# Block-sparse attention and a GELU feed-forward on one Trainium2 core: a reordered first unit, and all keys of a query block side by side

## The chip, the cores and the metric

The kernel runs on one core of a Trainium2 chip. Its engines are TensorE (PE, matrix products; its weight loads are listed as PEld), VectorE (DVE), ScalarE (ACT), GpSimd (POOL) and SyncE (SP, which here only issues transfers). Each engine works through its own queue of instructions in order, and semaphores hold an instruction back until what it needs is there. The metric is the device time of one execution in microseconds (us), lower is better. The first such time is given as the median of three runs.

## What is computed

Attention over 4 batches, 8 heads, 768 positions and 64 values per head, in blocks of 32 positions (24 blocks). Query block *i* sees key block *j* if they are at most one apart, if either is the first or the last block, or if *j* is one of three blocks drawn for *i* (`sampled_blocks`). The result goes through a feed-forward pair of products with an exact GELU between them.

```python
scores = q @ k.T / sqrt(64)
mask = |bi - bj| <= 1  or  bi in {0, 23}  or  bj in {0, 23}  or  bj in sampled_blocks[bi]
attn = softmax(where(mask, scores, -1e9)) @ v            # (4, 8, 768, 64)
x    = attn.transpose(0, 2, 1, 3).reshape(3072, 512)
h    = x @ w_in                                          # (3072, 2048)
out  = (0.5 * h * (1 + erf(h / sqrt(2)))) @ w_out        # (3072, 512)
```

Inputs and output are float32; inside, the kernel works in bfloat16 with float32 sums.

## The kernel before

**Units.** The work is cut into eight units (b, hf): batch b and half hf of its 24 query blocks, so (0,0), (0,1), (1,0) up to (3,1). Line 594 loops over them. Each unit has three stages: attention for 384 positions, FFN1 (the product with w_in and the GELU) and FFN2 (the product with w_out). Attention of one unit is interleaved with FFN2 of the unit before it, whose products are cut into 24 pieces by a generator (`ffn2_pieces`, L437) and are called in between. FFN1 stands alone, in eight steps (`ffn1_step`, L429), and the loading and transposing of the next batch is hung on these steps. The order on each engine is the order in which the program text issues instructions; nothing reorders it later.

**Groups.** A unit's attention has eight groups (`unit_groups`, L303): its dense block (the first or last query block, which sees all 768 keys) as two groups of four heads each, and eleven sparse blocks in pairs, the last one alone. A group goes through scores (L312), exp (L343), transposes of the probabilities (L356), their eviction from PSUM by ACT (L369), the products with V (`stage_av`, L376) and the transposes of the result into xT (L411). The loop at L486 runs these in a pipeline: in step `it` it does the V products of group it - 1, the transposes of group it, the scores of group it + 2 and the exp of group it + 1, with pieces of FFN2 between. In the first unit, which has no FFN2 to mix in, V products lag by three.

**Keys.** kT holds all keys of a batch transposed; two buffers alternate. For a sparse query block the 256 keys are its window of three neighbouring blocks (96 columns, read straight from kT), the three sampled blocks and the first and last block (160 columns, copied side by side into `kg`). `k_globals` (L243) copies the first and last block for all eleven query blocks of a unit at once; `k_sampled` (L250) copies one sampled block with a block number held in a register, on DVE or on POOL. `block_numbers` loads such registers of an engine from a small list.

**Values.** V is written with a column of ones into a scratch tensor in device memory (`v_scratch`, L257), from which each query block fetches its 256 rows: a window of 96 rows (`v_window`, L282, four query blocks to one transfer in the first unit) and three sampled blocks of 32 rows (`v_sampled`, L264), issued on SP or on POOL by which of the two holds the register. Rows of the first and last block are copied in by `v_ends` (L270). In the first unit `first_rows` and `first_values` (L565, L568) make the scratch copy of V and issue all fetches of units (0,0) and (0,1), the rest of w_in, w_out and the keys of batch 1; the table `extra` (L591) says at which step of attention they run. Elsewhere the fetches of a unit are issued one unit ahead.

**PSUM.** Scores and FFN1 share two buffers of two banks (psA), transposes two (psT), FFN2 has one bank (psO), the V products one (psV). ACT and DVE take FFN2's three output tiles of a unit from psO (L447).

Of the kernel before, what the change touches and what calls it, by code (L numbers as in the profile page):

```python
# [11 lines left out]
BF16 = mybir.dt.bfloat16  # L12
# [8 lines left out]
def kernel(  # L21
# [68 lines left out]
    kTs = [const.tile([P, NPR, S], BF16, name=f"kT{i}") for i in range(2)]  # L90
    kg = const.tile([P, US, NPR, 160], BF16, name="kg")
    vg0s = [const.tile([P, US, VR], BF16, name=f"vg0{i}") for i in range(2)]
# [150 lines left out]
    def k_globals(b, p0=0, p1=NPR):  # L243
        for c0, blk in ((96, 0), (128, NB - 1)):
            nc.vector.tensor_copy(
                kg[:, :, p0:p1, c0:c0 + BL],
                kTs[b % 2][:, None, p0:p1, blk * BL:(blk + 1) * BL].to_broadcast(
                    [P, US, p1 - p0, BL]))

    def k_sampled(b, js, vals, copy):  # L250
        for j in js:
            for r in range(NR):
                if (j, r) in vals:
                    copy(kg[:, (j - 1) % US, :, BL * r:BL + BL * r],  # L254
                         kTs[b % 2][:, :, bass.ds(vals[j, r] * BL, BL)])
# [56 lines left out]
    def stage_scores(b, hf, grp):  # L312
        qT, kT = qTs[b % 2], kTs[b % 2]

        def product(out_, h, j, rhs):
            rows = slice(64 * (h % 2), 64 * (h % 2) + 64)
            nc.tensor.matmul(out_, lhsT=qT[rows, h // 2, j * BL:(j + 1) * BL], rhs=rhs[rows],  # L317
                             start=True, stop=True)
        A = psA.tile([P, 1024], F32, name="sc", tag="A")
        nm = small.tile([P, 4], F32, name="nm")  # L320
        if grp[0] == "sparse":
            js = grp[1:]
            A4 = A.rearrange("p (g j c) -> p j g c", j=2, g=2)
            for i, j in enumerate(js):
                for c0, c1 in ((0, 96), (96, 256)):
                    for hh in range(4):
                        rhs = (kT[:, hh, (j - 1) * BL:(j + 2) * BL] if c0 == 0
                               else kg[:, (j - 1) % US, hh, :])
                        for G in range(2):
                            product(A4[32 * hh:32 * hh + 32, i, G, c0:c1], 2 * hh + G, j, rhs)  # L330
            n = len(js)
            nc.vector.tensor_reduce(out=nm[:, 0:2 * n].rearrange("p (j g) -> p j g", g=2),  # L332
                                    in_=A4[:, 0:n], op=ALU.max, axis=AX.X, negate=True)
        else:
            _, j, G = grp
            for c0, c1 in ((0, 512), (512, 768)):
                for hh in range(4):
                    product(A[32 * hh:32 * hh + 32, c0:c1], 2 * hh + G, j, kT[:, hh, c0:c1])
            nc.vector.tensor_reduce(out=nm[:, 0:1], in_=A[:, 0:S], op=ALU.max, axis=AX.X,  # L339
                                    negate=True)  # L340
        st[grp] = (A, nm)
# [95 lines left out]
    def ffn2_pieces(b, hf):  # L437

        for t in range(UT // P):
# [6 lines left out]
            os = opool.tile([P, D_MODEL], F32, name="os")  # L446
            if t == 1:  # L447
                nc.vector.tensor_copy(os, op)
            else:
                nc.scalar.copy(os, op)  # L450
            row = b * S + hf * UT + t * P
# [24 lines left out]
    def attention(b, hf, filler, extra, steps=(), lag=1):  # L476
# [9 lines left out]
        for it in range(-1, n + lag + 1):  # L486
            if it == -1:
                pieces(2)
                stage_scores(b, hf, groups[1])
                stage_exp(groups[0])  # L490
                pieces(3)
            else:
# [23 lines left out]
        for f in steps:  # L516
# [8 lines left out]
    nc.vector.tensor_copy(rf, ids)  # L525
    k_list = numbers_list(ids, J0[5:], RS, POOL)
    k_pool = registers(k_list)
# [3 lines left out]
    lists = [numbers_list(vf, J0[:6], (0, 1), SP), numbers_list(vf, J0[6:], (0,), SP),  # L531
             numbers_list(vf, J1, (0, 1), SP)]
    v_pool = block_numbers(vf, J0[:6], (2,), POOL) | block_numbers(vf, J0[6:], (1, 2), POOL)
# [4 lines left out]
    def k_unit(hf, b, js):  # L538
        if hf:
            k_sampled(b, js, k_pool, nc.gpsimd.tensor_copy)  # L540
        k_sampled(b, js, k_dve, nc.vector.tensor_copy)
# [8 lines left out]
    banks = [(psA, "A"), (psA, "A"), (psO, "O"), (psA, "A")]  # L550
    for half in (0, 1):
        for pr in (2 * half, 2 * half + 1):
            prep_pair(0, "k", pr, pr != 2, bank=banks[pr])
            prep_pair(0, "q", pr, True, 0, 64)
        if half == 0:
            k_globals(0, 0, 2)
    k_globals(0, 2, 4)
    k_dve = block_numbers(ids, J0[:5], RS, DVE)
    stage_scores(0, 0, unit_groups(0)[0])
    k_sampled(0, J0[5:], k_pool, nc.gpsimd.tensor_copy)  # L560
    k_unit(0, 0, J0[:2])
    load_w_in(1)
    v_ends(0, 0, nc.gpsimd.tensor_copy)

# [3 lines left out]
    def first_values():  # L568
# [3 lines left out]
        for a in range(0, US, 4):  # L572
            v_window(0, 0, a, min(a + 4, US))
            for j in J0[a:a + 4]:
                for r in range(NR):
                    v_sampled(0, j, r)
            if a < 8:
                load_w_in(2 + a // 4)
        for hs in HALVES:
            load_q(0, hs, slice(64, P))  # L580
        for part in (0, 1):
            load_w_out(part)
        v_pool.update(block_numbers(vf, J1, (2,), POOL))
        for a in range(0, US, 4):
# [4 lines left out]
        for hs in HALVES:  # L589
            load_k(1, hs)  # L590
    extra = {-1: [first_rows], 0: [first_values, lambda: k_unit(0, 0, J0[2:4])],  # L591
             1: [lambda: k_unit(0, 0, J0[4:5])]}

    for u in range(-1, len(units)):
        nxt = units[u + 1] if u + 1 < len(units) else None
        filler = iter(())
        if u >= 0:
            b, hf = units[u]
            fresh = nxt is not None and nxt[1] == 0
            if u == 0:  # L600
                k_dve |= block_numbers(ids, J1, (2,), DVE)
                k_pool = block_numbers(ids, J1, (0, 1), POOL)
            if nxt and not fresh:
                k_unit(1, b, J1)
            if u == 1:
                v_rows(1, nc.vector.tensor_copy)
                v_scratch(1)
                v_ends(1, 0, nc.gpsimd.tensor_copy)
                for f in sum(v_fetch(1, 0), []):
                    f()  # L610
# [15 lines left out]
            else:  # L626
                steps, later = [], []
            steps = iter(steps)
            for s in range(KOUT // 2):
                if s == KOUT // 2 - 1 and nxt:  # L630
                    stage_scores(*nxt, unit_groups(nxt[1])[0])
                ffn1_step(2 * s)
                next(steps, lambda: None)()
                if u == 0 and 3 <= s < 7:
                    prep_pair(0, "q", s - 3, False, 64, P)
                if u == 0 and s == 6:
                    k_dve |= block_numbers(ids, J0[5:], RS, DVE)
                    for f in load_qk(1)[2:] + load_v(1):
# [3 lines left out]
                if fresh and s < 4:  # L642
                    for pr in (2 * (s % 2), 2 * (s % 2) + 1):
                        prep_pair(b + 1, "k" if s < 2 else "q", pr, s >= 2)
                    if s == 1:
                        k_globals(b + 1)
                        k_unit(0, b + 1, J0)
            for f in steps:
                f()
            if nxt:  # L650
                nc.scalar.activation(warm, identity[:, 0:1], AF.Exp)
            filler = ffn2_pieces(b, hf)
        if nxt is None:
# [35 lines left out]
```

## Time and profile before

| what | value |
|---|---|
| median of three runs | 353.23 us (348.99 to 356.44) |
| the profiled execution | 352.86 us, of which the span from the first to the last instruction is 351.2 us |
| mean granted PE clock | 0.917 of full speed |
| busy: PE | 294.2 us (84%), weight loads 176.4 us |
| busy: ACT | 212.2 us (60%) |
| busy: DVE | 188.1 us (54%) |
| busy: POOL | 131.3 us (37%) |
| chain that ended last | PE 67%, ACT 12%, DMA 7%, "issue" 7%, DVE 3% |
| score products (L317) | 704 of 96 columns, 704 of 160 columns, 128 dense |
| start of FFN1 in the first unit | 53.83 us |

A page of the profile covers one execution. An engine's busy share is the time in which it executes something; register loads, branches and the issuing of transfers do not count as busy. A low share does not mean slack where an engine waits for another that waits for it. The chain that ended last is followed back from the last instruction, at each step to what released it; it says which work set the end. "issue" in it is time in which an engine stood still although it waited for nothing that the profile shows. Groups of instructions carry the line of the kernel, the engine, the operation and the tiles (out<-in) with their shape.

### The profile page before, as it was taken

To read this page: it belongs to the slowest core of one execution; us is meant where nothing else is said; L and a number is where in the kernel's file an instruction comes from. 1 tells how busy PE (TensorE), PEld (TensorE's weight loads), DVE (VectorE), ACT (ScalarE), POOL (GpSimd) and SP (SyncE) were. 2 spreads that over 40 slices of the span, in tenths; PEclk is the share of its full clock that TensorE was granted. 3 is DMA by queue.
4 is the path that set the end of the run, shared out by engine and by line. 5 is a ranking of instruction groups with operands and counts; after the bars stand their busy time and mean duration, and the time that the engine had idled before them with its cause. 6 is when DMAs were issued, how large, how long until landed. Compare 5 with 4: busy or idle time off the path is not lost.

```text
span 351.2 us, 13168 instructions
## 1 busy us (share of the span) xinstructions
PE 294.2 (84%) x5228; PEld 176.4 (50%) x5284; DVE 188.1 (54%) x561; ACT 212.2 (60%) x452; POOL 131.3 (37%) x269
## 2 busy tenths in 40 slices
PE   5536649986999889987699999996999989988996
PEld 4324424544555454544455464554564555455575
DVE  7397332566475656347457586346574674277000
ACT  2357322486647856578537795586657894688440
POOL 8383751184517644196630240596400410000000
PEclk9656556999699989999899999999999999999999
DMA  7945999979448972679954021798270120000002
GB/s 111 196 66 169 203 235 223 171 103 182 71 165 189 194 174 79 215 132 219 161 140 104 2 72 57 223 170 174 74 192 20 38 69 33 0 34 34 30 20 73
DMA packets 43807, 42.27 MB, mean 120 GB/s; under 512 B 7969, under 2 KB 38690, under 8 KB 43746
## 3 DMA queue, kind: packets, MB, share of 16 engines
q0 software_dynamic: 22528, 17.55, 31.8%
q1 hardware_dynamic: 20786, 23.48, 23.7%
q8 instruction: 41, 0.67, 0.8%
q10 hardware_dynamic: 432, 0.39, 0.3%
q14 instruction: 20, 0.16, 0.2%
HBM read 45.63 MB, written 9.67 MB: 157 GB/s over the span
## 4 chain that ended last, share of the span: by engine, by line
PE 67%; ACT 12%; DMA 7%; issue 7%; DVE 3%; SPq 1%; POOL 1%; DVEq 1%; POOLq 0%
PE hp L433 25%; PE op L442 18%; PE tp L365 6%; ACT pp L350 5%; PE av L392 5%; PE sc L317 4%; PE pt L227 4%; DMA vg<-vscr 4%; PE op L466 3%; ACT ps L372 2%; ACT L510 2%; DMA qn<-in_q_dram 2%; PE tx L422 2%; ACT g L435 1%; DMA vscr<-vn 1%
## 5 line engine op out<-in xcount | busy, mean ns | idle before, releaser
L433 PE MATMUL hp<-xT,w_in_sb 128*128 128x384 bf16 x512 | 91.0, 333 | 3.1 <-ACT g L435 2.8
L442 PE MATMUL op<-w_out_sb,g 128*128 128x512 bf16 x280 | 83.5, 390 | 11.5 <-issue 7.2
L435 ACT ACTIVATE g<-hp 128x768 bf16<-128x768 f32 x64 | 51.9, 810 | 56.2 <-PE hp L433 56.2
L268 POOL DMA_DIRECT2D vg<-vscr x108 | 54.0, 503 | 78.4 <-issue 24.9
L332 DVE TENSOR_REDUCE nm<-sc 128x4 f32<-128x1024 f32 (+1 forms) x48 | 54.5, 1135 | 32.1 <-PE sc L317 20.6
L350 ACT ACTIVATE pp<-sc,nm 128x256 bf16<-128x256 f32 x176 | 70.3, 497 | 0.0
L433 PEld LDWEIGHTS <-w_in_sb 128*128 128x128 bf16 x512 | 49.6, 99 | 39.6 <-issue 9.4
L372 ACT COPY ps<-tp 128x256 int32<-128x256 int32 (+2 forms) x128 | 39.9, 352 | 38.6 <-PE tp L365 37.2
L365 PE MATMUL tp<-identity,pp 128*128 128x128 bf16 x448 | 43.8, 238 | 7.3 <-ACT pp L353 4.1
L365 PEld LDWEIGHTS <-pp 128*128 128x128 bf16 x448 | 33.5, 112 | 29.1 <-ACT pp L353 11.2
L254 POOL COPY kg<-kT 128x128 bf16 x106 | 26.1, 293 | 58.5 <-PE sc L317 51.8
L339 DVE TENSOR_REDUCE nm<-sc 128x1 f32<-128x768 f32 x16 | 15.3, 957 | 43.9 <-PE sc L317 40.2
L442 PEld LDWEIGHTS <-g 128*128 128x128 bf16 x336 | 24.7, 98 | 23.7 <-issue 7.2
L392 PEld LDWEIGHTS <-ps 128*32 128x32 bf16 x1792 | 20.2, 99 | 28.6 <-issue 14.7
L392 PE MATMUL av<-vg,ps 128*32 128x65 bf16 x1408 | 23.0, 202 | 13.7 <-DMA vg<-vscr 7.2
L317 PE MATMUL sc<-kT,qT 64*32 64x96 bf16 (+2 forms) x832 | 26.3, 237 | 0.9 <-DVE qT L241 0.3
L405 DVE TENSOR_TENSOR xh<-av,rec 128x256 bf16<-128x256 f32 (+1 forms) x64 | 22.9, 358 | 2.2
L425 DVE COPY xT<-tx 128x256 bf16<-128x256 bf16 (+1 forms) x56 | 15.0, 267 | 16.5 <-PE tx L422 16.5
L317 PEld LDWEIGHTS <-qT 64*32 64x32 bf16 x1536 | 14.4, 93 | 18.2 <-issue 12.5
L317 PE MATMUL sc<-kg,qT 64*32 64x160 bf16 x704 | 18.5, 244 | 5.3 <-DVE kg L254 4.2
L398 DVE TENSOR_SCALAR den<-av 128x4 f32<-128x4 f32 (+1 forms) x64 | 10.0, 156 | 22.0 <-PE av L392 21.1
L450 ACT COPY os<-op 128x512 f32<-128x512 f32 x14 | 8.4, 601 | 19.4 <-PE op L442 19.4
(68 smaller groups left out, 273.0 us busy)
## 6 DMA issues: line engine op xcount, KB each, us to landing
vg<-vscr SPq DMA_DIRECT2D x20, 297.0 KB, 4.8
out_dram<-os SPq DMA_DIRECT2D x21, 256.0 KB, 2.1
vg<-vscr SPq DMA_DIRECT2D x156, 33.0 KB, 4.0
vg<-vscr POOLq DMA_DIRECT2D x108, 33.0 KB, 4.4
kn<-in_k_dram POOLq DMA_DIRECT2D x8, 384.0 KB, 5.6
vx<-in_v_dram POOLq DMA_DIRECT2D x8, 384.0 KB, 8.2
vscr<-vn SPq DMA_DIRECT2D x3, 792.0 KB, 3.4
qn<-in_q_dram POOLq DMA_DIRECT2D x6, 384.0 KB, 6.6
```

The costliest lines, as they stand in the source:

```text
L254: copy(kg[:, (j - 1) % US, :, BL * r:BL + BL * r], kTs[b % 2][:, :, bass.ds(vals[j, r] * BL, BL)])
L268: queue.dma_start(out=dst, in_=vscr[b][bass.ds(val * BL, BL), :])
L317: nc.tensor.matmul(out_, lhsT=qT[rows, h // 2, j * BL:(j + 1) * BL], rhs=rhs[rows], start=True, stop=True)
L332: nc.vector.tensor_reduce(out=nm[:, 0:2 * n].rearrange("p (j g) -> p j g", g=2), in_=A4[:, 0:n], op=ALU.max, axis=AX.X, negate=True)
L350: nc.scalar.activation(pp[:, 256 * n:256 * n + 256], A[:, c:c + 256], AF.Exp, bias=nm[:, n:n + 1])
L365: nc.tensor.transpose(T[:, c - c0, :], pp[:, cols], identity)
L372: nc.scalar.copy(ps[:, c0:c1, :].rearrange("p c k -> p (c k)").bitcast(I32), T[:, 0:c1 - c0, :].rearrange("p c k -> p (c k)").bitcast(I32))
L392: nc.tensor.matmul(av[32 * hh:32 * hh + 32, s, :], lhsT=probs[:, 32 * hh:32 * hh + 32], rhs=vals[:, VW * h:VW * h + D + 1], start=(c == 0) ...
L405: nc.vector.tensor_tensor(xh[:, at:at + n, :], av[:, 0:n, 0:D], rec[:, 0:n, None].to_broadcast([P, n, D]), op=ALU.mult)
L433: nc.tensor.matmul(hp[:, i, 0:UT], lhsT=w_in_sb[:, ki, (m + i) * P:(m + i + 1) * P], rhs=xT[:, ki, :], start=(ki == 0), stop=(ki == KIN - 1))
L435: nc.scalar.activation(g[:, m:m + 2, :], hp[:, :, 0:UT], AF.Gelu)
L442: nc.tensor.matmul(op, lhsT=g[:, m, t * P:(t + 1) * P], rhs=w_out_sb[:, m, :], start=(m == 0), stop=(m == KOUT - 1))
```

## The change

- **Keys side by side.** kg grows from 160 to 256 columns per head and query block: the window's 96 columns are now copied into it as well, by a new function `k_window` with three copies per unit on DVE, and sampled and global blocks move up by 96 columns. The scores of a query block are then one product of 256 columns per head instead of one of 96 and one of 160. The first unit keeps the two products and has no window copy.
- **First unit.** All K pairs are transposed before the Q halves, and evicted by ACT and DVE in turn. `first_rows` and `first_values` move ahead of the second dense group's scores (a new place -2 in `extra`). The end rows of V (`v_ends`) go from POOL to DVE. POOL copies the sampled keys of the first six query blocks, DVE those of the last five, whose register load moves into the attention loop. w_in's second part is loaded behind the first value rows.
- **Which engine does which list.** In first halves (hf 0) POOL now copies 18 of the 33 sampled key blocks and DVE 15 (before: DVE all, but for the first unit); in second halves POOL 15 and DVE 18 (before 22 and 11). All sampled V blocks of second halves are issued on SP (before, 11 of 33 on POOL). The end rows of unit (1,0) are copied from step 6 of the attention before.
- **FFN2.** The first piece is issued ahead of the last FFN1 step, so two instead of three pieces follow the second dense group's scores. The second output tile of a unit is evicted by ACT instead of DVE.

```diff
-    kg = const.tile([P, US, NPR, 160], BF16, name="kg")
+    kg = const.tile([P, US, NPR, 256], BF16, name="kg")
...
+    def k_window(b, hf):
+
+        for i in range(3):
+            t0 = (US * hf + i) * BL
+            nc.vector.tensor_copy(
+                kg[:, :, :, BL * i:BL * i + BL],
+                kTs[b % 2][:, :, t0:t0 + US * BL].rearrange("p r (u c) -> p u r c", c=BL))
...
-                for c0, c1 in ((0, 96), (96, 256)):
+                for c0, c1 in ((0, 96), (96, 256)) if (b, hf) == (0, 0) else ((0, 256),):
                     for hh in range(4):
-                        rhs = (kT[:, hh, (j - 1) * BL:(j + 2) * BL] if c0 == 0
-                               else kg[:, (j - 1) % US, hh, :])
+                        rhs = (kT[:, hh, (j - 1) * BL:(j + 2) * BL] if c1 == 96
+                               else kg[:, (j - 1) % US, hh, c0:])
...
-            if t == 1:
-                nc.vector.tensor_copy(os, op)
-            else:
-                nc.scalar.copy(os, op)
+            nc.scalar.copy(os, op)
...
                 pieces(2)
+                for f in extra.get(-2, ()):
+                    f()
                 stage_scores(b, hf, groups[1])
                 stage_exp(groups[0])
-                pieces(3)
+                pieces(2)
...
-    k_list = numbers_list(ids, J0[5:], RS, POOL)
+    k_list = numbers_list(ids, J0[:6], RS, POOL)
...
-             numbers_list(vf, J1, (0, 1), SP)]
+             numbers_list(vf, J1, RS, SP)]
...
     def k_unit(hf, b, js):
-        if hf:
-            k_sampled(b, js, k_pool, nc.gpsimd.tensor_copy)
+        k_sampled(b, js, k_pool, nc.gpsimd.tensor_copy)
         k_sampled(b, js, k_dve, nc.vector.tensor_copy)
...
-    for half in (0, 1):
-        for pr in (2 * half, 2 * half + 1):
-            prep_pair(0, "k", pr, pr != 2, bank=banks[pr])
-            prep_pair(0, "q", pr, True, 0, 64)
-        if half == 0:
-            k_globals(0, 0, 2)
+    for pr in range(NPR):
+        prep_pair(0, "k", pr, pr % 2 == 0, bank=banks[pr])
+    for pr in range(NPR):
+        prep_pair(0, "q", pr, True, 0, 64)
+    k_globals(0, 0, 2)
     k_globals(0, 2, 4)
-    k_dve = block_numbers(ids, J0[:5], RS, DVE)
     stage_scores(0, 0, unit_groups(0)[0])
-    k_sampled(0, J0[5:], k_pool, nc.gpsimd.tensor_copy)
-    k_unit(0, 0, J0[:2])
-    load_w_in(1)
-    v_ends(0, 0, nc.gpsimd.tensor_copy)
+    k_sampled(0, J0[:6], k_pool, nc.gpsimd.tensor_copy)
...
-            if a < 8:
-                load_w_in(2 + a // 4)
+            load_w_in(1 + a // 4)
...
-        v_pool.update(block_numbers(vf, J1, (2,), POOL))
...
-    extra = {-1: [first_rows], 0: [first_values, lambda: k_unit(0, 0, J0[2:4])],
-             1: [lambda: k_unit(0, 0, J0[4:5])]}
+    k_dve = {}
+    extra = {-2: [first_rows, first_values],
+             -1: [lambda: v_ends(0, 0, nc.vector.tensor_copy)],
+             0: [lambda: k_dve.update(block_numbers(ids, J0[6:], RS, DVE))],
+             1: [lambda: k_sampled(0, J0[6:8], k_dve, nc.vector.tensor_copy)],
+             2: [lambda: k_sampled(0, J0[8:], k_dve, nc.vector.tensor_copy)]}
...
             if u == 0:
-                k_dve |= block_numbers(ids, J1, (2,), DVE)
-                k_pool = block_numbers(ids, J1, (0, 1), POOL)
+                k_dve |= block_numbers(ids, J1[5:], RS, DVE)
+                k_pool |= block_numbers(ids, J1[:5], RS, POOL)
+                extra = {6: [lambda: v_ends(1, 0, nc.gpsimd.tensor_copy)]}
             if nxt and not fresh:
+                k_window(b, 1)
                 k_unit(1, b, J1)
...
                 if s == KOUT // 2 - 1 and nxt:
                     stage_scores(*nxt, unit_groups(nxt[1])[0])
+                    next(filler)
                 ffn1_step(2 * s)
...
                         k_globals(b + 1)
+                        k_window(b + 1, 0)
                         k_unit(0, b + 1, J0)
```

More of the change, by code (lines that the diff above doesn't have):

```diff
@@ L243, in k_globals @@
     def k_globals(b, p0=0, p1=NPR):
-        for c0, blk in ((96, 0), (128, NB - 1)):
+        for c0, blk in ((192, 0), (224, NB - 1)):
             nc.vector.tensor_copy(
@@ L253, in k_sampled @@
                 if (j, r) in vals:
-                    copy(kg[:, (j - 1) % US, :, BL * r:BL + BL * r],
+                    copy(kg[:, (j - 1) % US, :, 96 + BL * r:128 + BL * r],
                          kTs[b % 2][:, :, bass.ds(vals[j, r] * BL, BL)])
@@ L607 @@
                 v_scratch(1)
-                v_ends(1, 0, nc.gpsimd.tensor_copy)
                 for f in sum(v_fetch(1, 0), []):
@@ L628 @@
             steps = iter(steps)
+            filler = ffn2_pieces(b, hf) if nxt else None
             for s in range(KOUT // 2):
@@ L636 @@
                 if u == 0 and s == 6:
-                    k_dve |= block_numbers(ids, J0[5:], RS, DVE)
                     for f in load_qk(1)[2:] + load_v(1):
@@ L651 @@
                 nc.scalar.activation(warm, identity[:, 0:1], AF.Exp)
-            filler = ffn2_pieces(b, hf)
         if nxt is None:
```

## The prediction

> **What bounds the kernel now.** I read the page first: the span in slices, then the chain that ended last in order of time, then the timeline of one quiet unit and the waits.
>
> The span in slices:
>
> ```profile
> PE   5536649986999889987699999996999989988996
> PEclk9656556999699989999899999999999999999999
> DMA  7945999979448972679954021798270120000002
> ```
>
> TensorE (PE) is the bound except in the first six slices (8.8 us each), where it is half idle at a low clock. Its low slices later on fall where DMA is high. So there are two stages: a first unit that waits, and a steady part in which PE waits little.
>
> The chain in order of time (start, length, what), first unit:
>
> ```profile
> 15.19 1.80 DVEq L208
> 17.94 1.21 DVE kg L254 x6
> ...
> 21.73 3.67 DVE vn L129
> 25.84 4.91 DMA vscr<-vn
> 32.03 1.22 SPq L268
> 36.33 6.71 DMA vg<-vscr
> 43.06 6.90 DMA vg<-vscr
> ```
>
> FFN1 cannot start (53.83) until the last value rows have been fetched from the scratch copy of V, and that scratch is written only at 25.4, because VectorE (DVE) first loads registers (1.80), copies keys (1.21) and then needs 3.67 for a copy whose neighbour of the same shape takes 0.83 on ScalarE (ACT): GpSimd (POOL) holds a 4.80 copy (L280, from 20.32) over the same time.
>
> The same chain later on, the four longest "issue" pieces:
>
> ```profile
> 84.80 2.69 issue
> ...
> 122.14 1.78 issue
> ...
> 166.29 2.25 issue
> ...
> 242.78 2.38 issue
> ```
>
> PE stands still for nothing that it waits on. With a fifth, 0.96 at 161.66, these are 10.1 us. The DMA view of 84.8 to 87.5 shows one 16 KB packet of the instruction queue in it; all 41 such packets are 0.67 MB, 256 instructions of 64 B each, and PE's 10,570 instructions make 41.3 such blocks. The stalls lie in the units (0,1), (1,0), (1,1), (2,1), with a DMA share of 0.69 to 0.86; attention there takes 28.8, 27.0, 28.0, 25.4 us, and 23.0, 22.9, 22.9 in (2,0), (3,0), (3,1), where the share is 0.07 to 0.14. Excess: 17.2 us, the stalls and what they draw after them (a clock of 0.88 to 0.94, late refills).
>
> The timeline of quiet unit (2,0), a sparse step and the tail (start, length, engine, what, idle before):
>
> ```profile
> 206.95 0.24 PE L317 MATMUL sc<-kT,qT 64*32 64x96 bf16 x8
> 207.30 0.61 PE L442 MATMUL op<-w_out_sb,g 128*128 128x512 bf16 x2
> 207.32 1.58 ACT L350 ACTIVATE pp<-sc,nm 128x256 bf16<-128x256 f32 x4
> 209.17 0.66 ACT L372 COPY ps<-tp 128x256 int32<-128x256 int32 x2 [0.27 <-PE tp L365]
> ...
> 211.48 0.68 DVE L448 COPY os<-op 128x512 f32<-128x512 f32 x1
> 212.22 0.59 PE L442 MATMUL op<-w_out_sb,g 128*128 128x512 bf16 x2 [0.57 <-DVE os L448]
> 212.86 1.28 ACT L510 ACT_TABLE_LOAD   x1
> 214.26 0.41 ACT L372 COPY ps<-tp 128x128 int32<-128x128 int32 x2
> ```
>
> A step lasts 2.40; ACT works 2.13 to 2.24 of it and idles 0.16 to 0.27, PE is nearly full. In the tail ACT runs without a pause from 211.46 into the table load and the last eviction (214.26), and PE's next transpose (214.56) needs the buffer which that frees.
>
> **The change part by part,** against the profiled execution: span 351.2, time 352.9 (1.7 around it), 0.4 below the median 353.2.
>
> *First unit.* DVE's new queue: its list work ends at 9.25; two K evictions (0.95 each) 11.2; four global copies (0.31 to 0.35) 12.5. The dense scores need Q: its data arrive at 10.40, four ACT copies of 0.50 make it 12.9, scores (0.85) 13.7, maximum (0.96) 14.7. Then both V copies, 0.74 and about 0.4. V itself: issued by 6.81, median landing 8.2, so 15.0, and ACT's 0.83 after that. ACT now stands at that copy with the first exp queued behind it: exp at about 16, before 18.06. The scratch writes go out at about 16.5 instead of 25.4; the POOL copy is gone. From there the fetch has the same order on SP and the same number of transfers on POOL (16 value rows, two w_in parts between them), so FFN1 starts 8.8 earlier, at 45. Ends: 9.6 (no wait for V) and 6.5 (w_in part 1, issued before at 18.85 in an emptier stretch, now lies among the rows: 512 KB at 225 GB/s are 2.3). I take 8.8: that part replaces part 2 at the same place. Moved behind it on DVE: end rows (0.29 and 1.52), the register load (1.80), 15 key copies (0.11 to 0.20). They delay the sparse maxima, but the first sparse value product waits for rows until about 27 in any case; without that cover they cost up to 5.
>
> *Right after.* POOL's w_out loads, issued at 48.14 before, come 8.8 earlier less 0.8 for the issue of w_in part 3 ahead of them, so at 40. Before, both halves took until about 68 (POOL's wait for them ends at 68.44), 20 us; the second is first read at 72.1 (L442's fifth product after 71.26). Now 40 + 20 + 2.3 for part 3 is 62, perhaps 65, and it is read at 62.9. +1.0 (0 to 3.5).
>
> *Score products.* 1,408 become 792: 616 products and as many weight loads fewer, with the same columns. 32 products take 0.35 from first to next work, so 10.9 ns each if count alone decides (6.7 in all), nothing if columns do. In a step the first eight 96-column products start at 206.95 and the next eight at 207.07, with eight of 160 between: 256 columns on each of eight tiles in 0.12. Eight products of L442 take 1.90 with the last 0.38 long, 0.217 apart for 512 columns, so 0.109 for 256. Columns decide: 0.02 for each of 39 groups, -0.7. The Trainium skill, TensorEngine Tiling (Array Packing), section Instruction Overhead, gives about 60 cycles per matmul; at the 2.4 GHz of its page Trainium Kernel Development and Optimization that is an estimated 25 ns, 15.4 us in all, and the sum would be 325.9. The trace speaks against it: 10.9 ns a product with its columns.
>
> *Instruction blocks.* A sparse step goes from 156 PE instructions to 124, so 256 of them last 3.94 before and 4.95 after, and a late block stalls 1.0 less: 1.7, 0.8, 0, 1.25, 1.4 are left of the five, -4.9. Of the 7.1 that follows the stalls I take 2.1. Together -7.0 (0 to -17.2). The Trainium skill, Runtime: NRT & Kernel Launch, section Instruction fetch mechanics, has blocks of 256 instructions too, the next one fetched during the current, at a cost mostly hidden; the packets agree with the size, the stalls not with the hiding. By it this term is nothing.
>
> *Second output tile on ACT.* In the tail ACT takes 0.62 more and loses its 0.16 idle: +0.46 in seven units, +3.2. PE's 0.57 wait for DVE goes, but PE then waits at the transpose, so no credit. Ends: -2.0 (PE alone sets the tail, 0.3 each) and +4.3.
>
> *Nothing.* One op piece now fills the six gaps of 0.44 before the last FFN1 step, yet the first transpose still waits for gelu 0.81, table 1.28 and exp 0.88; if not, -2.6. Window copies: three of 0.88 for each of seven units on DVE, in FFN1: 3.6 more than before with second halves, where DVE idles 5.85, 0.8 more with first halves, where it idles 2.34. POOL's new 18 copies (4.55) stand behind 16 row issues in (1,0), ending at 114.5; the first six are done at 116, needed at 118.7. Where they wait for K, POOL's V loads stand behind them, due a unit later. SP gets 44 row issues from POOL, 11 in a unit; at 0.6 to 0.98 they push the output rows and the scratch write behind them from 141.8 to 152 at most, with rows due at 203. If these covers fail, up to 3 each.
>
> Sum: 351.2 - 8.8 + 1.0 - 0.7 - 7.0 + 3.2 = 338.9; with 1.7 around it, 340.6.
>
> **The rivals.**
> 1. The late blocks stay late (a fetch stands in full DMA queues whatever PE's count): without the 7.0, 347.6. For: DMA bytes are the same, and the stall at 242.78 had a half-empty DMA. Against: a longer block is time in any case. 0.22. By the Trainium skill's section Instruction fetch mechanics, too, the count of instructions would be worth nothing.
> 2. Products cost by their number: -6.7 instead of -0.7, 334.6. For: ACT has 0.16 to 0.27 a step to give. Against: the column spacing above. 0.10. The Trainium skill's section Instruction Overhead points this way.
> 3. w_out lands no earlier than before (68 instead of 62.9, so 3.7 of the 8.8 is left; 1.0 is counted already): 344.7. For: DMA share 1.10 in that stretch. 0.10.
> 4. Slower: ACT, strictly in order, reaches the second tile's copy before PE has finished it. The page's other output copies wait 2.8 each (19.4 in 7); with the copy 3.4 instead of 0.46 in seven units, 361.2. It decides from 2.8 us of wait on. Against: in (2,0) that product ends at 211.20, ACT's exp at 211.29. 0.08.
>
> **How the numbers follow.** My forecast has 0.50, with 334 to 346 from the ends of its terms. The range: rival 2 and more of the 17.2 reach down to 331; rival 1 with a shorter first gain up to 352; left out are rival 4 and some 0.1 at the edges. The three runs lie 2.1% apart, so 2% is about what can be told: faster is below 346.2, slower above 360.3. Faster: 0.46 of the forecast, rival 2, 0.08 of rival 3, 0.06 of rival 1: 0.70. Slower: 0.08. Within: 0.22.
>
> **What would show it.** Scratch writes at 16 to 17 and FFN1 at 44 to 46 (first unit); "issue" stalls of 4 to 6 in all; 32 columns' products replaced by 16 in about 0.33; the last evictions 0.5 later after the exp in each tail; no PE wait on kg. Wrong if the first FFN1 starts after 48, if stalls grow, or if ACT waits over 1 us for the second tile.

## The result, and the profile after

The changed kernel takes 329.83 us (median of 4 runs, 329.46 to 331.1) where the kernel before took 351.97 in runs on the same chip (4 runs, 348.99 to 356.44): a ratio of 0.940 with a 95% interval of 0.933 to 0.948. One of those four runs of before, 356.44, is a slow one and is left out of this ratio, as slow runs are in the ratios further on. The forecast was 340.6 with a range of 331 to 352, so the direction was right, but the time lies 1.2 below the range and the gain of 21 to 22 us is nearly twice the 12 to 13 foretold. The profiled execution has a span of 327.9 us against 351.2, 23.3 less.

The span in 40 slices (here 8.2 us each), kernel after:

```profile
PE   5568689998999989988999989998999989998995
PEclk9555569999999999999999999999999999999999
DMA  7969999991578835995664313995540310011001
```

TensorE (PE) is still half idle at a low clock at the start, but from the seventh slice on it stays at 8 or 9 until the last. The dips to 6 and 7 of before are gone, although DMA is about as busy as it was: its share is 0.69 to 0.87 before and 0.69 to 0.81 after in the attention of (0,1), (1,0), (1,1) and (2,1). The granted clock over these four is 0.88, 0.94, 0.94 and 1.00 before, and 1.00 in all of them after.

The chain that ended last, in order of time (start, length, what): first unit, and the one stall of PE in attention.

```profile
6.04 10.52 DMA vx<-in_v_dram
16.58 0.84 ACT vn L129
17.45 3.55 DMA vscr<-vn
22.26 1.09 SPq L276
...
27.43 6.72 DMA vg<-vscr
34.16 5.64 DMA vg<-vscr
...
43.55 7.10 PE hp L442 x32
...
146.76 0.97 issue
```

VectorE (DVE) is no longer in the first unit's chain. V's arrival (16.58) now sets the scratch write, and FFN1 starts at 43.55 instead of 53.83. Of five stalls of 10.1 us in all, one of 0.97 is left on the chain (PE's own timeline has a second one of 0.52, at 111.29). Pieces of 0.67 that the chain of after also calls "issue" lie in six tails, during ACT's table load, and are not counted here.

The timeline of the quiet unit (2,0) (start, length, engine, what, idle before), with one scores product of unit (0,1) ahead of it:

```profile
71.62 0.41 PE L325 MATMUL sc<-kg,qT 64*32 64x256 bf16 x16
71.96 0.60 PE L451 MATMUL op<-w_out_sb,g 128*128 128x512 bf16 x2
...
187.62 1.58 ACT L359 ACTIVATE pp<-sc,nm 128x256 bf16<-128x256 f32 x4
...
189.09 0.59 ACT L456 COPY os<-op 128x512 f32<-128x512 f32 x1
...
189.58 0.65 ACT L381 COPY ps<-tp 128x256 int32<-128x256 int32 x2
...
190.11 0.87 ACT L359 ACTIVATE pp<-sc,nm 128x256 bf16<-128x256 f32 x2
...
190.99 1.28 ACT L518 ACT_TABLE_LOAD   x1
...
192.39 0.41 ACT L381 COPY ps<-tp 128x128 int32<-128x128 int32 x2
192.69 0.27 PE L431 MATMUL tx<-identity,xh 128*128 128x128 bf16 x2 [0.71 <-ACT ps L381]
```

Sixteen products of 256 columns take 0.34 from their start to the next work (71.62 to 71.96); the 32 of before took 0.35. ScalarE (ACT) takes the second output tile with no wait in front of it, is then busy without a pause into the table load, and PE waits 0.71 for its last eviction; before, PE waited 0.57 for DVE at the tile instead.

Where the 23.3 us come from can be read off the starts of FFN1. "Attention" here runs from the start of the last FFN1 product of a unit to the start of the first one of the next; by this measure the seven stages of before are up to 0.4 off the ones the prediction gave. All in us, one profiled execution each; the lower rows are the experiments of the next section.

| kernel | first FFN1 | attention in (0,1) | (1,0) | (1,1) | (2,0) | (2,1) | (3,0) | (3,1) | sum of the seven |
|---|---|---|---|---|---|---|---|---|---|
| before | 53.8 | 28.4 | 26.7 | 28.3 | 23.3 | 25.8 | 23.2 | 23.2 | 178.9 |
| after | 43.6 | 23.4 | 24.2 | 24.6 | 23.4 | 23.7 | 23.4 | 23.4 | 166.1 |
| e1_two_products | 43.2 | 25.4 | 27.2 | 25.6 | 23.5 | 23.8 | 23.5 | 23.5 | 172.5 |
| e2_three_products | 44.3 | 25.8 | 29.1 | 28.1 | 24.4 | 26.8 | 23.8 | 24.3 | 182.3 |
| e3_before_merge | 54.6 | 25.4 | 25.1 | 23.8 | 23.2 | 23.7 | 23.3 | 23.2 | 167.7 |
| e4_before_rows | 53.9 | 26.6 | 25.0 | 25.1 | 23.3 | 25.5 | 23.2 | 23.2 | 171.9 |
| e5_before_first | 45.1 | 29.3 | 27.0 | 26.6 | 23.3 | 24.7 | 23.3 | 23.2 | 177.3 |
| e6_before_ends | 53.1 | 26.1 | 26.4 | 26.6 | 23.3 | 24.9 | 23.2 | 23.2 | 173.8 |
| e7_tile_dve | 44.0 | 23.6 | 24.8 | 24.1 | 23.2 | 23.6 | 23.1 | 23.1 | 165.4 |
| e8_no_early | 44.6 | 23.4 | 24.1 | 23.4 | 23.4 | 23.7 | 23.4 | 23.4 | 164.9 |
| e9_first_merge | 43.1 | 28.2 | 26.9 | 23.9 | 23.2 | 23.2 | 23.1 | 23.1 | 171.6 |
| e10_fm_rows01 | 45.1 | 23.3 | 26.8 | 24.3 | 23.1 | 24.2 | 23.1 | 23.1 | 167.9 |
| e11_before_rows01 | 54.9 | 26.7 | 27.0 | 26.7 | 23.3 | 25.6 | 23.3 | 23.2 | 175.8 |

The first unit gives 10.3 us and the seven attention stages 12.8. The quiet stages, (2,0), (3,0) and (3,1), are 0.1 to 0.2 longer than before; all of the 12.8 comes from the four that were slow. The prediction had 8.8 and, net, 3.5. Each row is one execution: e8, which differs from after only in an early piece, is 1.2 away from it in (1,1), so a difference of about 1 us in one slow stage says little. The execution profiled of e10 took 333.37, which is 3.3 above its median, and that of e11 351.16, 2.1 above.

### The profile page after: what moved, and what is told of

The parts are those of the page before. It is cut to its first block, busy times and chain, and to the rows that moved or that the text cites. A ratio compares the mean times of both kernels' runs of the same rounds, so it can differ in the third digit from the quotient of the medians.

```text
span 327.9 us, 11961 instructions
## 1 busy us (share of the span) xinstructions
PE 294.6 (90%) x4668; PEld 167.6 (51%) x4668; DVE 196.0 (60%) x550; ACT 214.0 (65%) x458; POOL 112.4 (34%) x249
## 3 DMA queue, kind: packets, MB, share of 16 engines
q1 hardware_dynamic: 22898, 24.97, 26.6%
## 4 chain that ended last, share of the span: by engine, by line
PE 57%; ACT 23%; DMA 11%; issue 4%; SPq 2%; POOL 1%; DVE 1%; POOLq 0%
PE hp L442 27%; PE op L451 12%; ACT pp L359 9%; DMA vg<-vscr 6%; PE tp L374 4%; ACT ps L381 3%; PE av L401 3%; PE pt L227 3%; PE sc L325 3%; DMA vx<-in_v_dram 3%; PE op L472 3%; ACT L658 3%; SPq L276 2%; ACT g L444 2%; ACT pp L362 2%
## 5 line engine op out<-in xcount | busy, mean ns | idle before, releaser
L451 PE MATMUL op<-w_out_sb,g 128*128 128x512 bf16 x336 | 94.6, 382 | 1.3 <-ACT os L456 1.3
L276 POOL DMA_DIRECT2D vg<-vscr x64 | 32.2, 505 | 67.6 <-DMA vscr<-vn 30.8
L262 POOL COPY kg<-kT 128x128 bf16 x132 | 34.5, 315 | 50.1 <-DVE kT L237 27.6
L374 PEld LDWEIGHTS <-pp 128*128 128x128 bf16 x448 | 31.1, 107 | 32.4 <-ACT pp L362 14.8
L451 PEld LDWEIGHTS <-g 128*128 128x128 bf16 x336 | 23.9, 97 | 23.9 <-issue 10.9
L456 ACT COPY os<-op 128x512 f32<-128x512 f32 x21 | 12.6, 599 | 19.6 <-PE op L451 19.6
L401 PE MATMUL av<-vg,ps 128*32 128x65 bf16 x1408 | 21.4, 201 | 2.8 <-issue 1.5
L431 PE MATMUL tx<-identity,xh 128*128 128x128 bf16 x96 | 15.2, 229 | 8.0 <-ACT ps L381 4.9
L431 PEld LDWEIGHTS <-xh 128*128 128x128 bf16 x96 | 9.1, 98 | 22.0 <-DVE xh L414 8.2
L325 PE MATMUL sc<-kg,qT 64*32 64x256 bf16 (+1 forms) x704 | 19.7, 282 | 0.0
L237 DVE COPY kT<-pt 128x768 bf16<-128x768 bf16 x14 | 12.8, 952 | 7.6 <-PE pt L227 7.6
```

What stands on the lines that cost most here:

```text
L262: copy(kg[:, (j - 1) % US, :, 96 + BL * r:128 + BL * r], kTs[b % 2][:, :, bass.ds(vals[j, r] * BL, BL)])
L276: queue.dma_start(out=dst, in_=vscr[b][bass.ds(val * BL, BL), :])
L374: nc.tensor.transpose(T[:, c - c0, :], pp[:, cols], identity)
L401: nc.tensor.matmul(av[32 * hh:32 * hh + 32, s, :], lhsT=probs[:, 32 * hh:32 * hh + 32], rhs=vals[:, VW * h:VW * h + D + 1], start=(c == 0) ...
L431: nc.tensor.transpose(T[:, i, :], xh[:, 2 * i:2 * i + 2, :].rearrange("p g d -> p (g d)"), identity)
L451: nc.tensor.matmul(op, lhsT=g[:, m, t * P:(t + 1) * P], rhs=w_out_sb[:, m, :], start=(m == 0), stop=(m == KOUT - 1))
```

## The experiments

Each ratio is to the kernel before on the same chip, whose medians were 350.76 (e1 to e4), 351.39 (e5 to e8), 351.14 (e9) and 353.01 (e10, e11).

**How many instructions PE has in a step.** In e1 the kernel after goes back to two products per query block and head in all units (156 instructions of PE in a sparse step), in e2 it has three except in the first unit (188), with the same 256 columns. The window copies into kg are still made, but these two kernels read the window from kT.

```diff
-  for c0, c1 in ((0, 96), (96, 256)) if (b, hf) == (0, 0) else ((0, 256),):
+  for c0, c1 in ((0, 96), (96, 256)):                                                  # e1
+  for c0, c1 in ((0, 96), (96, 256)) if (b, hf) == (0, 0) else ((0, 96), (96, 176), (176, 256)):  # e2
...
-                               else kg[:, (j - 1) % US, hh, c0:])
+                               else kg[:, (j - 1) % US, hh, c0:c1])
```

> The changed kernel with two score products per head again in every unit (96 columns from kT, 160 from kg); the window copies stay, unused. PE has its 1,232 instructions back. Theory 1 (a longer block of 256 instructions hides the late fetch): the issue stalls come back in the units (0,1), (1,0), (1,1), (2,1), 6 to 10 us of them, attention there 25 to 28 us instead of 23.7, 23.9, 24.3, 23.5; time 338 to 344. Theory 2 (the transfers that moved from POOL to SP, and the loads that go out earlier, keep the fetch from being late): nothing or up to 2 us, 330 to 332. In the quiet units both expect 23.1 to 23.3, as columns decide what the products cost.

> The changed kernel with three score products per head (96, 80, 80 columns) outside the first unit: 188 PE instructions a sparse step instead of 124 or 156, the same columns. Theory 1: a block lasts 3.3 us, stalls of 12 us or more, time 343 to 350, and even the quiet units lose a little where delay plus 2.4 us is over 3.3. Theory 2: 330 to 333. If products cost by number: 4 to 7 us more than with two products also in the quiet units.

Measured: 336.95 (ratio 0.963, 0.955 to 0.970) and 347.5 (0.992, 0.988 to 0.996), after 329.83 with one product. The first is just below the 338 to 344 of the theory of late blocks and far from the 330 to 332 of the other; the second lies inside the 343 to 350 of the first theory. The chain of e1 shows three stalls of over 1 us inside attention, that of e2 six:

```profile
68.98 1.69 issue
111.67 1.95 issue
...
151.10 1.97 issue
```

```profile
69.81 1.90 issue
110.40 1.11 issue
115.12 2.59 issue
...
152.50 1.95 issue
...
233.38 1.47 issue
238.45 1.23 issue
```

That is 5.6 and 10.3 us, against 0.97 with one product. In the table, e1 loses 6.0 of its 6.4 us in the units (0,1), (1,0) and (1,1), and 0.1 in each quiet one. A quiet unit has 88 products more in e1, so about 1 ns for each product with its weight load. From one product to two, what costs time is therefore neither the products nor their columns but the number of instructions, and nearly all of it where DMA is busy. With three products the quiet units lose as well, 0.4 to 1.0 each, without a stall of over 0.4; why is not shown.

How a block stalls can be worked out by counting PE's instructions in the trace, 256 to a block, and setting the packets of the instruction queue beside the count. When PE crosses into a block, the packet of the block after it is still to come. If it comes late and the block in hand is used up, PE stands still. In the five stalls of before the packet started 3.5 to 4.6 after the crossing, the block in hand lasted 3.7 to 4.9 to the end of its last instruction, and work went on 2.3 to 2.8 after the packet's start. In (2,1) before, 3.51 + 2.53 - 3.67 gives the stall of 2.37; in (1,1) after, 3.83 + 2.29 - 5.12 gives 1.00, and 0.97 is in the trace.

Two things changed. The block in hand lasts longer, 5.1 where it stalls in after and in e3. And the ends of blocks meet other delays: in the seven attention stages PE crosses 28 block ends before and 23 after, and the packet starts over 3 us after the crossing at five of them before (3.51 to 4.55, all five stall), at two after (3.29 and 3.83) and at four in e3 (3.13 to 4.37, of which three fall on blocks of 5.6 or more). The latest fetches are thus nearly as late as ever, but fewer of them meet a block that is too short. Why the others come in time was not tested.

**The merge alone.** e3 is the kernel before with one product for the 256 columns and the window copies, and nothing else of the change.

```diff
+    def k_window(b, hf): ...
-                for c0, c1 in ((0, 96), (96, 256)):
+                for c0, c1 in ((0, 96), (96, 256)) if (b, hf) == (0, 0) else ((0, 256),):
...
+                k_window(b, 1)
                 k_unit(1, b, J1)
...
                         k_globals(b + 1)
+                        k_window(b + 1, 0)
```

> The kernel before with only the keys side by side (one product of 256 columns, window copies on DVE, first unit as before). Theory 1: stalls fall from 10.1 us to under 3, time 8 to 14 us less than before (338 to 344 by a before of 352). Theory 2: within 2 us of before.

Measured: 341.94 (ratio 0.976, 0.969 to 0.982), 8.8 less, as the theory of late blocks had it. Attention is 11.2 shorter in all. One stall of 1.71 that the chain calls "issue" is left in attention. A standstill of 2.0 at 73.17 in unit (0,1) is of another kind, as the waits between 55 and 84 us show (engine line, waited for: us in total, times, longest):

```profile
POOL vg L276 <- DMA w_out_sb<-in_moe_w_out_dram: 14.5, 2, 7.8
...
PE sc L325 <- POOL kg L262: 2.2, 2, 2.0
```

GpSimd (POOL) is held for 14.5 us at the issue of value rows until w_out has landed; the key copies stand behind these rows on POOL, and PE comes to wait for kg. The hold is part of the program: in the trace POOL's transfers signal eight semaphores in turn (99 to 106), and an issue waits until the transfer eight places ahead of it has landed. In before, the two halves of w_out land at 60.78 and 68.17, and the row issues that wait for their semaphores start at 61.06 and 68.44, 0.28 later each. The key copies for (0,1) come behind the last of them, and PE's first sparse scores hard upon these (timeline of before):

```profile
68.44 2.26 POOL L268 DMA_DIRECT2D vg<-vscr  x4 [6.89 <-DMA w_out_sb<-in_moe_w_out_dram]
70.76 1.57 POOL L103 DMA_DIRECT2D kn<-in_k_dram  x2
73.31 5.24 POOL L254 COPY kg<-kT 128x128 bf16 x22 [0.97 <-DVE nm L339]
...
73.59 0.24 PE L317 MATMUL sc<-kT,qT 64*32 64x96 bf16 x8
```

This led to the next runs.

**The value rows of second halves.** e4 is the kernel before with all sampled rows of second halves issued on SP, nothing else. e9 is the kernel before with the merge and the new first unit together, so that a third of these rows is still on POOL (it also keeps DVE for the second tile, has no early FFN2 piece, and splits the key copies as before).

```diff
-             numbers_list(vf, J1, (0, 1), SP)]
+             numbers_list(vf, J1, RS, SP)]
...
-        v_pool.update(block_numbers(vf, J1, (2,), POOL))
```

> The kernel before with only the value rows of second halves all issued on SP (44 issues leave POOL, so its loads of K, Q and V go out earlier). Theory 1: stalls stay at 8 to 12 us, within 3 us of before. Theory 2: 8 to 14 us less than before.

> The kernel before with the merged products and the new first unit, but with a third of the second halves' value rows still on POOL, the second tile on DVE and no early piece. Theory A (the two parts add up, and the moved rows carry their own share of about 5): 8.8 and 7.7 off the kernel before, 334 to 336, issue stalls of 2 to 4. Theory B (once a step has 124 instructions of PE the blocks come in time, whichever queue issues the rows): 328 to 331, stalls of at most 1.5.

Measured: e4 345.74 (ratio 0.986, 0.981 to 0.991), between what the theories gave; e9 335.45 (0.958, 0.952 to 0.965), 5.6 more than the kernel after. That is within the 334 to 336 of the theory by which the moved rows carry a share of their own; the theory that merged steps suffice gave 328 to 331. Only one stall over 1 us is left in the attention of e9 (2.11), so its loss is not mainly instructions. The timeline of e9 in unit (0,1) shows it:

```profile
53.40 1.81 POOL L276 DMA_DIRECT2D vg<-vscr  x1 [5.07 <-DMA w_out_sb<-in_moe_w_out_dram]
...
60.62 2.27 POOL L276 DMA_DIRECT2D vg<-vscr  x4 [5.41 <-DMA w_out_sb<-in_moe_w_out_dram]
62.94 1.58 POOL L103 DMA_DIRECT2D kn<-in_k_dram  x2
65.43 1.72 POOL L262 COPY kg<-kT 128x128 bf16 x7 [0.91 <-issue]
66.02 0.89 PE L325 MATMUL sc<-kg,qT 64*32 64x256 bf16 x16 [3.55 <-POOL kg L262]
```

Eleven row issues, two of them held 5 us each, end at 62.9, the loads of K follow, the key copies begin at 65.43, and PE has stood for 3.55 when the first are done. The issues that are held, at 53.40 and 60.62, are again the eighth ones behind the halves of w_out, which land at 53.12 and 60.34. FFN1 is over 10 us earlier than before, but the landing of w_out lets POOL go only 7.8 earlier (at 60.62 instead of 68.44). In the kernel after no row is issued there, and POOL copies keys from 47.24.

The same with only the 11 rows of unit (0,1) moved to SP, in e10 on top of e9 and in e11 on the kernel before:

```diff
-             numbers_list(vf, J1, (0, 1), SP)]
+             numbers_list(vf, J1, RS, SP)]
...
-        v_pool.update(block_numbers(vf, J1, (2,), POOL))
         for a in range(0, US, 4):
             ...
+        v_pool.update(block_numbers(vf, J1, (2,), POOL))
         for hs in HALVES:
             load_k(1, hs)
```

> The kernel of e9_first_merge with the 11 rows of unit (0,1) alone issued on SP; those of (1,1), (2,1), (3,1) stay on POOL. In e9, POOL's issues of these 11 rows stand 10.5 us behind the landing of w_out, the key copies of (0,1) behind them, and PE waits 3.5 for kg. Theory H (that hold is what the moved rows take away): 329 to 331.5, no wait of PE for kg over 0.5. Theory R (rows on POOL cost in every second half): 332 to 335, the attention of (1,1) and later as in e9 and that of (0,1) shorter by 3.5 at most.

> The kernel before with the 11 rows of unit (0,1) alone issued on SP. Theory H: as e4_before_rows, 345 to 347, with the shorter attention in (0,1) and (1,0), where POOL's loads of batch 1 are issued 10 us earlier. Theory R: 348 to 351, since 33 of the 44 rows are still on POOL.

Measured: e10 330.11 (ratio 0.937, 0.928 to 0.947), in theory H's range and not to be told from the kernel after; e11 349.02 (0.991, 0.986 to 0.996), in R's 348 to 351 by its median, while the interval of the ratio, 345 to 349 us, reaches into H's 345 to 347 as well. In e10 the copies start as soon as FFN1's first product lets them, and the hold and PE's wait for kg are gone:

```profile
48.81 6.31 POOL L262 COPY kg<-kT 128x128 bf16 x22 [5.89 <-PE hp L441]
```

The attention of (0,1) is 23.3 instead of 28.2, a gain of 4.9, where the wait for kg was 3.5. So with the early first unit the hold behind w_out is what the moved rows take away, and moving 11 of 44 is enough. On the kernel before, it is not all: e4 shortens (1,0) and (1,1) by 1.7 and 3.2, and e11 by -0.3 and 1.6 only, in single executions, that of e11 a long one. How rows of later second halves act there was not separated further.

**The first unit.** e5 is the kernel before with the first unit's new order alone; e6 with one piece of it, the end rows of V copied by DVE behind the value copies instead of by POOL beside them.

```diff
-    v_ends(0, 0, nc.gpsimd.tensor_copy)
...
-             1: [lambda: k_unit(0, 0, J0[4:5])]}
+             1: [lambda: k_unit(0, 0, J0[4:5])],
+             2: [lambda: v_ends(0, 0, nc.vector.tensor_copy)]}       # e6
```

> The kernel before with only the first unit's new order (K pairs ahead of Q, V's scratch copy ahead of the second dense scores, end rows on DVE, sampled keys of six blocks on POOL, w_in part 2 among the rows). Prediction's term: FFN1 of the first unit starts at 43.5 to 45 instead of 53.8, and time is 8 to 10 us less than before (about 341). Rival (w_out or the rows of (0,1) then come late and give it back): FFN1 as early, but time only 3 to 5 us less.

> The kernel before with only the end rows of the first unit (v_ends) copied by DVE in step 2 instead of by POOL ahead of the loop. If the 3.67 us of the V copy is a wait for POOL's 4.80 us copy: it takes 0.4 to 0.8, the scratch writes go out about 3.2 earlier (22.2), FFN1 starts at 50 to 51, time 2 to 3 us less. If the copy is slow for its own pattern: it stays at 3.67, FFN1 at 53 to 55, time within 1 us of before.

Measured: e5 343.72 (ratio 0.980, 0.973 to 0.988), 7.7 less where 8 to 10 was expected, with FFN1 at 45.1 and a wait of PE for kg of 1.26 in unit (0,1): the new first unit alone also meets POOL's late copies. e6 346.2 (0.987, 0.979 to 0.995). Its timeline of the first unit:

```profile
21.15 0.54 DVE L129 COPY vn<-vx 128x1536 bf16<-128x1536 bf16 x1
...
22.75 0.41 DVE L129 COPY vn<-vx 128x768 bf16<-128x768 bf16 x1
...
23.19 0.83 SPq L260 DMA_DIRECT2D vscr<-vn  x2
```

Without the POOL copy over it, the copy that took 3.67 takes 0.41 and the scratch write goes out at 23.19 instead of 25.43. By the Trainium skill, SBUF - State Buffer, section SBUF: two separate sides, one pair of ports is shared by GpSimd and those DVE operations that need it, as a lock held for a whole instruction. These two durations agree with that if this copy is such an operation, which no run here shows by itself. But FFN1 starts at 53.1, only 0.7 earlier, where 50 to 51 was expected: a scratch write 2.2 earlier does not bring the last rows earlier by as much; why was not traced. e6's gain of 5.2 is more than the 2 to 3 expected, and its edit does not explain it: by the table 5.0 of it lie in attention, 2.3 in (0,1) and 1.7 in (1,1). In that profile PE had its full clock from the start, as its slices show,

```profile
PEclk9999999999999999999999999999999999999999
```

where the profile of before had 0.50 between 44 and 54 us; FFN1 of (0,0) took 14.8 us in it, 15.8 in before. The clock alone is not the answer either: e6's other three executions, at a mean clock of 0.925 or 0.926, took 344.49 to 348.65, about the 346.28 of this one. So this part of e6 stays open.

**The tail and the early piece.** Both are the kernel after with one part undone.

```diff
-            nc.scalar.copy(os, op)
+            if t == 1:
+                nc.vector.tensor_copy(os, op)
+            else:
+                nc.scalar.copy(os, op)                # e7
...
-                    next(filler)
...
-                pieces(2)
+                pieces(3)                             # e8
```

> The changed kernel with the second output tile of FFN2 evicted by DVE again. Prediction's term (ACT sets the tail; the copy there costs 0.46 in each of seven units): 2 to 3.5 us less than the changed kernel, 326.5 to 328, PE's 0.71 wait at the tail's transposes shrinks to about 0.3. Rival (PE's wait for DVE's copy, 0.57, costs as much as ACT's): within 1 us of 329.8.

> The changed kernel without the early FFN2 piece (three pieces after the second dense scores again). Prediction's term (the first transposes wait for gelu, table load and exp either way): within 1 us of 329.8. Rival: the gap of 0.44 before the last FFN1 step comes back on the path, 2 to 3 us more (332 to 333).

Measured: e7 329.14 (ratio 0.938, 0.933 to 0.943) and e8 329.7 (0.939, 0.934 to 0.945): neither can be told from the kernel after by its time, where the prediction's term for the tile had e7 at 326.5 to 328. The profile of e7 tells more. Its quiet stages last 23.2, 23.1 and 23.1, 0.2 to 0.3 less than after, and the timeline of its tail in (2,0) is:

```profile
189.72 0.68 DVE L457 COPY os<-op 128x512 f32<-128x512 f32 x1
...
190.45 0.59 PE L451 MATMUL op<-w_out_sb,g 128*128 128x512 bf16 x2 [0.54 <-DVE os L457]
...
191.09 1.28 ACT L521 ACT_TABLE_LOAD   x1
...
192.79 0.27 PE L431 MATMUL tx<-identity,xh 128*128 128x128 bf16 x2
```

PE's wait of 0.54 for DVE is back and its 0.71 for ACT is gone; the net is the 0.2 to 0.3 of a unit. In e8, the first transposes of (2,0) start at 175.65 instead of 175.54, as late behind FFN1 as in after: there PE waits 0.40 for the first exp, and in e8 the third piece fills that time.

## Why the prediction came out too high

By its own steps, the profiled sum missed by 11.0: 338.9 was forecast for the span, 327.9 came.

- **First unit, -8.8: right in kind, 10.3 came (1.5 more).** V was ready at 16.58, later than the 15.0 taken from the median landing, and the scratch write went out at 17.04, where 16.5 was forecast. What was not counted is that the work behind it got shorter: the scratch transfer took 3.55 instead of 4.91 in the chain, and the last piece of row fetches 5.64 instead of 6.90. ACT stood 2.75 at the V copy with the first exp behind it, as forecast, and exp followed at 17.32.
- **w_out, +1.0: nothing came.** Its second half landed at 58.82, 9.4 earlier than before, and no wait of PE for w_out is seen in the first FFN2. Rival 3, w_out landing no earlier than before, fell with it.
- **Score products, -0.7: right.** Sixteen products of 256 columns take 0.34, 32 took 0.35, and e1's 88 further products in a quiet unit cost 0.1, where a price by number (10.9 ns each) gives 1.0. Rival 2 (cost by number) is refuted for the step from two products to one. So is what the Trainium skill, TensorEngine Tiling (Array Packing), section Instruction Overhead, gave: the 32 products with their columns took 10.9 ns a piece, far less than the estimated 25.
- **Second output tile on ACT, +3.2: right place, too large.** The undoing in e7 shows 0.2 to 0.3 in a quiet unit, so some 1.9 for seven. The 0.46 a unit had refused PE any credit for the wait that goes; in fact PE's waits are 0.71 against 0.57. Rival 4, ACT waiting for the second tile, did not happen: in (2,0) ACT passes to the copy without idling.
- **Instruction blocks, -7.0: the step that failed.** With the tail and the products taken off, the seven attention stages are 12.8 + 1.9 - 0.7 = 14.0 shorter, twice as much. The step said that "a late block stalls 1.0 less" and kept all five late blocks, so 5.2 of the 10.1 us of stalls were to be left; its own sign was "stalls of 4 to 6 in all". 0.97 is left on the chain. Of the 7.1 that follows the stalls the step took 2.1; what is left of the 14.0 beside 9.1 of stalls is 4.9, and the granted clock of 0.88 to 0.94 that went with them is 1.00 now. The 1.0 itself was not the error: with the lengths that the five blocks really had (3.7 to 4.9, and 5.1 after), the same working leaves 5.6. What was wrong is that the five late blocks were carried over from before, each with its delay, although the new program's blocks end at other instructions: after the change two packets in attention start over 3 late, not five. e3 shows it for the merge alone: one stall of 1.7 is left in attention, and attention there is 11.2 shorter, where this step and the products had 7.7. Rival 1 (late blocks stay late) gave 347.6 and fell by the same runs, although some fetches do stay late, by up to 3.83. It is also where the Trainium skill, Runtime: NRT & Kernel Launch, section Instruction fetch mechanics, by which a crossing is mostly hidden, does not hold as a price of nothing: with 124, 156 and 188 instructions in a step the otherwise equal kernels take 329.8, 337.0 and 347.5.
- **Nothing, for POOL's rows: a second term put too low.** The prediction priced the 44 moved row issues for SP, where they come, and at nothing for POOL, which they leave. It quoted the end of POOL's wait (68.44) only as the landing time of w_out. But in the trace of before POOL's key copies for (0,1) start at 73.31, behind that hold and the loads of K, and the first sparse scores at 73.59: a cover of next to nothing. With the rows left on POOL, an earlier first unit runs into it: e9 loses 4.9 in (0,1) to e10. So part of the first unit's 10.3 is kept only because the rows were moved.
- **Early piece and window copies, nothing: right** by e8 for the piece; no wait of PE for kg is seen in the kernel after, and e3's only one behind the first unit is for POOL's copies.

The parts do not simply add. Merge, rows and first unit alone give 8.8, 5.0 and 7.7, whose sum of 21.5 is close to the 22.1 measured; but merge and rows remove in part the same stalls (attention -11.2 and -7.0 alone), while rows and first unit need each other. That the sum fits is partly chance.

Still open: why fetches of instructions start 3 to 4.5 us after the crossing in some blocks and about 1 in others, and why fewer of them are late with the merged products; what gave e6 its gain in attention; and whether w_out issued behind the rows would have done as much as moving the rows. Attention in (1,0) is 26.8 in e10 and 24.2 in the kernel after: e10's profiled execution has a stall of 2.11 there at a clock of 0.94, after has one of 0.52 at 1.00, and as that execution is 3.3 above e10's median, this need not be a difference of the kernels.

## What to carry to other kernels

Before costing a part at nothing because it "moves off" an engine, look at what stands behind it in that engine's queue and how close its consumer is: a consumer that starts 0.28 after the first of its copies begins has no cover left once anything ahead gets faster. Where a long unrolled program stalls with no wait in the profile, count the instructions of the bound engine per unit of time, block by block; fewer, larger instructions can be worth several times their own execution time where DMA is busy, and little where it is not. When a term is a lateness that strikes where it exceeds a cover, do not carry the list of places over from the old trace: here five became two when the blocks ended elsewhere. And where an issue waits for a transfer that it does not use, look at the semaphores: here the one eight places ahead had to land first, so a large load among small ones holds what is queued behind it.

## What the runs showed of the hardware

PE resumed 2.3 to 2.8 us after the start of the late instruction packet: 2.30 to 2.78 in the five stalls of before, 2.29 in after, 2.30 to 2.55 in e1, 2.27 to 2.67 in the six of e2, 2.48 in e3. The granted clock of PE in the first unit differs between executions: 0.50 (before) and 1.00 (e6) over the same 10 us; FFN1 of (0,0), next to it, took 15.8 and 14.8 us. The waits of POOL's row issues for w_out, 13.3 us in the kernel before, 14.5 in e3 and 10.5 in e9, do not belong here: they are waits for semaphores that the program itself contains, and row issues on SP wait in the same way for earlier rows, for 3.0 at the longest in the kernel after.
